# Attention and two mixtures of experts on one core: softmax reciprocals by logarithm and exponential, one pair of maxima moved, low parts of outputs moved to VectorE

## The chip, the cores and the metric

The kernel runs on 1 core of one Trainium2 chip. The metric is device time in microseconds (us), the median of three runs. A core has five engines with instruction streams of their own, each in its written order: TensorE (PE in the rows; its weight loads are PEld), VectorE (DVE), ScalarE (ACT), GpSimd (POOL) and SyncE (SP), which issues DMAs. They wait for each other by semaphores. SBUF and PSUM are the on-chip memories; matmuls write to PSUM.

## The reference

```
attention: q,k,v (2 batches, 8 heads, 1152 rows, 64 wide), fp32
  q_pool = mean of each two rows of q               # 576 rows
  scores = q_pool @ k.T / sqrt(64);  scores -= max over keys
  attn   = exp(scores);  attn /= (sum over keys + 1e-9)
  out    = attn @ v                                 # becomes x, 1152 x 512
first mixture, 4 experts, dense:  x = sum_e p_e * (relu(x @ w1[e]) @ w2[e])
second mixture, 8 experts, each row goes to its best one, times its gate
```

## The kernel before

Every value that must keep fp32 precision is split into a high part (fp32r) and a low part, the difference of the two; a product is then three matmuls: high by high, low by high, high by low.

**Jobs.** Two heads make a pair p (eight pairs); a pair has two jobs, g = 2p with 256 query columns and g = 2p+1 with 320. Even and odd below mean g. The loop `for g in range(NG)` runs the sixteen jobs in a written order, without a scheduler (`tc.manual_schedule`). A job is:

- The stream (`streams`, with `score` and `smax1`). For each of 9 key blocks and each of the two heads, four matmuls (three products and the subtraction of the maximum, `mr` by `ones`) make a score tile S, and ScalarE takes its exponential into an E tile. The two heads use the two halves of TensorE's rows and run side by side. Between them stand matmuls for the maxima of later jobs: one writes a buffer T of 384 columns, and VectorE reduces it to a maximum (L109, L110). How S and maxima (m) alternate stands in the strings `PAT`, one for each head. There are five PSUM banks for S (four named S0 to S3 and O) and three buffers T, used in turn.
- Behind the stream (called the tail below): `mT` transposes the next job's maxima into a T, and ScalarE copies them to `mr` (L130, and for odd next jobs two small copies L132). After an even job come the three tail maxima (`tops`, `tmax`, L118) into S0, S1 and a T. After an odd job come the transposes of later keys and queries (`keys`; `kT`, L65, into S0, S1 and a T; `qT`, L97, into two T).
- Then `fin(g-2)` splits the output x of the job before the last into high and low part; the low part is made on VectorE for even jobs and on GpSimd for odd ones. Then the weighted sums `av` (L174): two key blocks, then `normalise(g-1)`, then the other seven. `normalise` calls `total`, four matmuls that sum the exponentials into a T called z (L177), which ScalarE copies to r with 1e-9 added (L179); `norm(g,1)`, two reciprocals of r on VectorE (L185); and `norm(g,2)`, the product x times r (L187). `norm(g,0)` copies the weighted sum O to x (L183).

GpSimd adds up the exponentials (L168) all through attention. The list `todo` gives each job its share of the maxima of later jobs: 5 for job 0, 7 for jobs 1 to 3, 6 for jobs 4 to 13, 3 for job 14, and none for the last; each is a pair, one matmul per head.

Job 14 runs all its weighted sums ahead of `normalise(13)`. After job 15 the weights of the first mixture are split (L279 on ScalarE, L282 on VectorE), its matmuls begin (L318 to L320, then ScalarE L322 and VectorE L323 on each result), and job 15's own normalisation runs in the midst of them (`end`). From there on the kernel is the two mixtures; the change doesn't touch them.

Of the kernel before, what the change touches and what calls it, by code (L numbers as in the profile page):

```python
# [9 lines left out]
def attention(tc, q, k, v, xT, identF, prep, begin, second, keep, NJ=16):  # L10

    nc=tc.nc
    B,H,S,D=q.shape
    Q=S//2; NC=S//128; NP=NJ//2; NG=2*NP
    PAT=(("SmSSmSmSSmSmSSm","mSmSSmSmSSmSmSS"),)*2+(("SmSmSmSSmSmSSmSm","mSmSSmSmSSmSmSSm"),)
    JOB=((0,256),(256,320))
    HD=(slice(0,64),slice(64,128))
    with ExitStack() as ctx:
# [4 lines left out]
        st={}  # L23
# [9 lines left out]
        def load(p):  # L33
            b,h0=divmod(2*p,H)
            kn=ld.tile([128,NC,2,D],F32,name="kn"); qn=ld.tile([128,2,5,2,D],F32,name="qn"); vn=vp.tile([128,2,NC,D],F32,name="vn")
            st['ld',p]=kn,qn; st['v',p]=vn
            def kload(c):
                for n in range(2): nc.sync.dma_start(kn[:,c,n],k[b,h0+n].rearrange("(p c) d -> p c d",c=NC)[:,c])
            def qload(e,i0,i1):
                for n in range(2):  # L40
                    e.dma_start(qn[:,n,i0:i1],q[b,h0+n,256*i0:256*i1].rearrange("(i p r) d -> p i r d",p=128,r=2))
                    if i1==4: e.dma_start(qn[:,n,4],q[b,h0+n,896:1152].rearrange("(p r) d -> p r d",r=2))
            if p==0:
                qload(nc.scalar,0,2)
                for c in range(3): kload(slice(3*c,3*c+3))
                qload(nc.sync,2,4)
            else:
                qload(nc.sync,0,4); kload(slice(0,9))
            if p>1: load_v(p)
# [63 lines left out]
        def smax(g,i,early=False):  # L113
            for h in range(2): smax1(g,i,h,early)
# [10 lines left out]
        def mT(g):  # L125
            p,u=divmod(g,2); M=MM[u]; n=2+u; o=JOB[u][0]
            mr=st['m',g]=kq.tile([128,JOB[u][1]],F32R,name=f"mr{u}")
            f=T1(384)
            for t in range(n): nc.tensor.transpose(f[:,t*128:(t+1)*128],M[:,t].rearrange("p h d -> p (h d)"),identF)
            nc.scalar.copy(mr[:,0:256],f[:,0:256])  # L130
            if u:
                for h in range(2): nc.scalar.copy(mr[HD[h],256:320],f[HD[h],256+64*h:320+64*h])  # L132
# [42 lines left out]
        def total(g,z=None):  # L175
            n=JOB[g%2][1]; z=T1(n) if z is None else z[:,0:n]
            for h in range(2): nc.tensor.matmul(z[HD[h]],ones4,st['es',g][:,h,0:n],start=True,stop=True)  # L177
            r=st['r',g]=keep['r'] if g==NG-1 else fp.tile([128,320],F32,name="r")
            nc.scalar.activation(out=r[:,0:n],in_=z,func=AF.Identity,bias=eps)  # L179
        def norm(g,n0):  # L180
            n=JOB[g%2][1]; r=st.get(('r',g)); x=st['x',g]
            if n0==0:
                nc.scalar.copy(x[:,0:n],st['O',g][:,0:n])  # L183
            if n0==1:
                for a in range(0,n,n//2): nc.vector.reciprocal(r[:,a:a+n//2],r[:,a:a+n//2])  # L185
            if n0==2:
                nc.vector.tensor_tensor(out=x[:,0:n],in0=x[:,0:n],in1=r[:,0:n],op=ALU.mult)  # L187
        def fin(g):
            p,u=divmod(g,2); o,n=JOB[u]; b,dc=divmod(p,H//2); x=st['x',g]
            g0=b*Q+o; g1=g0+n  # L190
            while g0<g1:
                m=g0//384; e=min(g1,(m+1)*384)
                src=x[:,g0-b*Q-o:e-b*Q-o]; xh,xl=xT[m]; sl=slice(g0-384*m,e-384*m)
                nc.scalar.copy(xh[dc][:,sl],src)
                (nc.vector if g==NG-1 or u==0 and g<NG-2 else nc.gpsimd).tensor_tensor(out=xl[dc][:,sl],in0=src,in1=xh[dc][:,sl].bitcast(F32),op=ALU.subtract)
                g0=e
        load(0)
        with tc.manual_schedule():
            dw=O1(320)
            def warm(n):  # L200
                for _ in range(n): nc.tensor.matmul(dw[:,0:128],identF,identF,start=True,stop=True)
            qsum(0,slice(0,2))
            load(1)
            warm(7)
            kT(0,0); warm(1)
            qlow=qT0(0); warm(1)
            smax(0,0,True); smax(0,1,True)
            kT(0,1); st['low',0](); qlow()
            smax(0,2,True); warm(2); smax(0,3,True)
            kT(0,2); st['low',1]()  # L210
            qsum(0,slice(2,5))
            smax(0,4,True); st['low',2]()
            warm(2)
            qlow=qT0(1)
            smax(0,5,True); qlow()
            load_v(0)
            neg(0); smax(1,0); warm(3); mT(0); warm(2)
            load_v(1)
            def normalise(g): total(g); norm(g,1); norm(g,2)
            todo=[(j,i) for j in range(1,NG) for i in range(6)][1:]  # L220
            for g in range(NG):
                p,u=divmod(g,2); last=g==NG-1
                n=(5,7,7,7)[g] if g<4 else 6
                rl,todo=todo[:n],todo[n:]
                if g==0: qsum(1)
                elif u==0 and p+2<NP: load(p+2)
                elif g==NG-4: begin()
                elif u and p+2<NP: qsum(p+2)
                def between(c,hh,i):
                    if hh==1 and i==3 and c==4 and last: fin(g-2)  # L230
                streams(g,range(NC),rl,PAT[n-5],between)
                if last: break
                r=1 if g==0 else p+2 if u else NP
                def keys():
                    if r<NP:
                        for n in range(3): kT(r,n,S1(n,384) if n<2 else None)
                        qT(r)
                def tops(p):
                    if p<NP:
                        for c in range(3): tmax(p,c,S1(c,384) if c<2 else None)  # L240
                if g==0:
                    tops(0); neg(1)
                    keys(); load(2)
                    av(g,0,4); mT(1); av(g,4,NC)
                else:
                    mT(g+1)
                    if g==1: tops(1)
                    if u==0: tops(p+1)
                    keys()
                    if g>1: fin(g-2)  # L250
                    if g==NG-2: prep[0][2](); prep[3][1]()
                    c=NC if g==NG-2 else 2
                    av(g,0,c); normalise(g-1)
                    if g==NG-3:
                        for i in range(3): prep[i][1]()
                    if g==NG-2: prep[1][2]()
                    av(g,c,NC)
                norm(g,0)
            g=NG-1
            prep[2][2](); prep[3][2]()  # L260
            kqx.close(); second()
            av(g,0,NC); normalise(g-1); norm(g,0); fin(g-1)
# [635 lines left out]
```

## Time and profile before

| What | us |
|---|---|
| median of 3 runs (lowest, highest) | 773.88 (773.84, 775.05) |
| the profiled execution | 772.89 |
| its span in the profile | 771.1 |
| TensorE busy in the span | 756.8 (98%) |
| VectorE, ScalarE, GpSimd busy | 395.4, 315.0, 247.9 |

The profile is of one execution. Times in its rows count from the span's start. Attention takes the first 222 us; there VectorE is busy some 17 to 18 of every 20 us and GpSimd about 19, and in the mixtures TensorE alone is near full. Matmuls are pipelined: two that follow each other overlap in the records, so TensorE looks busy where it stalls for a few tenths, and steps from start to start tell more than durations. TensorE's granted clock is 1.00 of full speed throughout attention.

### The profile page before, as it was taken

To read this page: it belongs to the slowest core of one execution; us is meant where nothing else is said; L and a number is where in the kernel's file an instruction comes from. 1 tells how busy PE (TensorE), PEld (TensorE's weight loads), DVE (VectorE), ACT (ScalarE), POOL (GpSimd) and SP (SyncE) were. 2 spreads that over 40 slices of the span, in tenths; PEclk is the share of its full clock that TensorE was granted. 3 is DMA by queue.
4 is the path that set the end of the run, shared out by engine and by line. 5 is a ranking of instruction groups with operands and counts; after the bars stand their busy time and mean duration, and the time that the engine had idled before them with its cause. 6 is when DMAs were issued, how large, how long until landed. Compare 5 with 4: busy or idle time off the path is not lost. (4 is left out here: it accounts for less than half of the span.)

```text
span 771.1 us, 13240 instructions
## 1 busy us (share of the span) xinstructions
PE 756.8 (98%) x5166; PEld 636.9 (83%) x5166; DVE 395.4 (51%) x826; ACT 315.0 (41%) x734; POOL 247.9 (32%) x216
## 2 busy tenths in 40 slices
PE   8999999999999999999999999999999999999995
PEld 7778787877778989899898989989797978878773
DVE  6798898899594102521125212243252678474610
ACT  4757676766762212511124201132141454473611
POOL 5889999999993000000000000000000201311001
PEclk9999999999999999999999999999999999999999
DMA  8532133220063000420004000000154142797891
GB/s 225 128 97 78 20 96 98 74 97 2 9 187 134 1 1 1 158 88 1 1 0 140 26 1 1 0 1 1 42 192 151 42 164 96 274 327 301 330 371 68
DMA packets 57640, 77.54 MB, mean 101 GB/s; under 512 B 22935, under 2 KB 33175, under 8 KB 57568
## 3 DMA queue, kind: packets, MB, share of 16 engines
q1 hardware_dynamic: 55136, 70.76, 27.5%
q0 software_dynamic: 1600, 4.98, 1.9%
q8 instruction: 43, 0.70, 0.4%
q10 hardware_dynamic: 832, 0.85, 0.3%
q14 instruction: 29, 0.24, 0.1%
HBM read 71.86 MB, written 4.98 MB: 100 GB/s over the span
## 5 line engine op out<-in xcount | busy, mean ns | idle before, releaser
L322 ACT ACTIVATE hh<-ps 128x384 fp32r<-128x384 f32 x96 | 47.1, 491 | 203.9 <-PE ps L320 203.9
L318 PE MATMUL ps<-xb,w 128*128 128x384 f32 x384 | 129.6, 337 | 0.4 <-DVE hl L323 0.4
L320 PE MATMUL ps<-xb,w 128*128 128x384 f32 x384 | 128.6, 335 | 0.0
L323 DVE SCALAR_TENSOR_TENSOR hl<-ps,hh 128x384 fp32r<-128x384 f32 x96 | 53.4, 557 | 146.2 <-ACT hh L322 145.9
L468 POOL TENSOR_TENSOR r_n<-r_ss,half 128x1 f32<-128x1 f32 x9 | 5.3, 593 | 375.5 <-ACT X L467 375.5
L333 PE MATMUL py<-w,hh 128*128 128x512 f32 x288 | 112.8, 392 | 0.0
L335 PE MATMUL py<-w,hl 128*128 128x512 f32 x288 | 112.8, 392 | 0.0
L334 PE MATMUL py<-w,hh 128*128 128x512 f32 x288 | 112.7, 391 | 0.0
L319 PE MATMUL ps<-xc,w 128*128 128x384 f32 x288 | 96.7, 336 | 0.0
L282 DVE TENSOR_TENSOR w<-st,w 128x1024 fp32r<-128x1024 f32 x60 | 78.0, 1324 | 36.3 <-ACT w L279 35.2
L110 DVE TENSOR_REDUCE m<-T 128x1 f32<-128x384 f32 x180 | 88.9, 548 | 11.9 <-PE T L109 9.6
L168 POOL TENSOR_TENSOR y<-y,E 128x640 f32<-128x640 f32 x56 | 92.5, 1652 | 4.3
L143 ACT ACTIVATE E<-S 128x256 f32<-128x256 f32 (+1 forms) x240 | 84.7, 414 | 8.5 <-PE S L140 7.6
L168 POOL TENSOR_TENSOR es<-es,E 128x512 f32<-128x512 f32 x56 | 74.7, 1333 | 4.4
L174 PE MATMUL O<-E,vn 128*64 128x320 f32 (+1 forms) x576 | 75.8, 409 | 0.0
L279 ACT CAST w<-st 128x1024 fp32r<-128x1024 f32 x60 | 61.4, 1051 | 35.2 <-PE py L335 22.2
L318 PEld LDWEIGHTS ps<-xb,w 128*128 128x128 f32 x384 | 72.1, 188 | 1.9 <-issue 0.8
L320 PEld LDWEIGHTS ps<-xb,w 128*128 128x128 f32 x384 | 72.1, 188 | 0.0
L342 DVE SCALAR_TENSOR_TENSOR y<-py,p,y 128x512 f32<-128x512 f32 x27 | 20.2, 749 | 87.5 <-PE py L335 87.5
L140 PE MATMUL S<-qh,kh 64*128 64x256 f32 (+1 forms) x240 | 64.0, 303 | 0.2 <-ACT E L143 0.2
L140 PE MATMUL S<-qh,kl 64*128 64x256 f32 (+1 forms) x240 | 63.5, 301 | 0.0
L334 PEld LDWEIGHTS py<-w,hh 128*128 128x128 f32 x288 | 54.1, 188 | 11.3 <-issue 0.6
(398 smaller groups left out, 1591.4 us busy)
## 6 DMA issues: line engine op xcount, KB each, us to landing
st<-in_moe_w SPq DMA_DIRECT2D x104, 512.0 KB, 6.3
kn<-in_k SPq DMA_DIRECT2D x14, 288.0 KB, 4.6
vn<-in_v SPq DMA_DIRECT2D x14, 288.0 KB, 3.4
qn<-in_q SPq DMA_DIRECT2D x14, 256.0 KB
ysc<-y SPq DMA_DIRECT2D x9, 256.0 KB, 2.0
qn<-in_q SPq DMA_DIRECT2D x16, 64.0 KB, 4.0
kn<-in_k SPq DMA_DIRECT2D x6, 96.0 KB, 3.0
vn<-in_v ACTq DMA_DIRECT2D x2, 288.0 KB
```

Of the source, the lines that this page charges most:

```text
L110: nc.vector.tensor_reduce(out=m[:,t,h,c:c+1],in_=s,axis=AX.X,op=ALU.max)
L140: nc.tensor.matmul(s,l[hd],r[hd],start=i==0,stop=i==3)
L143: nc.scalar.activation(out=st['E',g,c][:,h,0:n],in_=s,func=AF.Exp)
L168: nc.gpsimd.tensor_tensor(out=s,in0=st['E',g,0][:,:,0:n] if c==1 else s,in1=st['E',g,c][:,:,0:n],op=ALU.add)
L174: for h in range(2): nc.tensor.matmul(O[HD[h],0:n],vn[:,h,c],st['E',g,c][:,h,0:n],start=c==0,stop=c==NC-1)
L282: def low(): (nc.vector if le=='V' else nc.gpsimd).tensor_tensor(out=wl,in0=st,in1=wh.bitcast(F32),op=ALU.subtract)
L318: nc.tensor.matmul(ps,wh[:,fs],xh[dc],start=(dc==0),stop=False)
L319: nc.tensor.matmul(ps,wh[:,fs],xl[dc],start=False,stop=False)
L320: nc.tensor.matmul(ps,wl[:,fs],xh[dc],start=False,stop=(dc==3))
L333: nc.tensor.matmul(py,hh[:,us],wh[:,cs],start=(fc==0),stop=False)
L334: nc.tensor.matmul(py,hh[:,us],wl[:,cs],start=False,stop=False)
L335: nc.tensor.matmul(py,hl[:,us],wh[:,cs],start=False,stop=(fc==7))
```

## The change

Four things are changed, all in `attention`. (1) `total` no longer copies z to r: ScalarE takes the logarithm of z + 1e-9 and then the exponential of its negative, an approximate reciprocal. `norm(g,1)` refines it by a Newton step in two VectorE instructions, the first of which writes into z, in PSUM; what they leave is the negative of the reciprocal, and `norm(g,2)` turns the sign with the product. One ScalarE function table that holds both functions is loaded at the start. (2) Of a job's pairs of maxima the last one (the sixth, or the seventh in jobs 1 to 3) is issued behind `mT` instead of in the stream; job 0, and job 14 with three, keep all in the stream. (3) The strings PAT are spaced for five or six pairs. (4) `fin` makes the low parts of jobs 1 to 11 of odd number on VectorE too; jobs 13 and 14 stay on GpSimd.

```diff
--- before.py
+++ after.py
@@ -12,7 +12,7 @@
     nc=tc.nc
     B,H,S,D=q.shape
     Q=S//2; NC=S//128; NP=NJ//2; NG=2*NP
-    PAT=(("SmSSmSmSSmSmSSm","mSmSSmSmSSmSmSS"),)*2+(("SmSmSmSSmSmSSmSm","mSmSSmSmSSmSmSSm"),)
+    PAT=(("SmSSmSSmSSmSSm","mSSmSSmSSmSSmS"),("SmSSmSmSSmSmSSm","mSmSSmSmSSmSmSS"))
     JOB=((0,256),(256,320))
     HD=(slice(0,64),slice(64,128))
     with ExitStack() as ctx:
@@ -176,15 +176,19 @@
             n=JOB[g%2][1]; z=T1(n) if z is None else z[:,0:n]
             for h in range(2): nc.tensor.matmul(z[HD[h]],ones4,st['es',g][:,h,0:n],start=True,stop=True)
             r=st['r',g]=keep['r'] if g==NG-1 else fp.tile([128,320],F32,name="r")
-            nc.scalar.activation(out=r[:,0:n],in_=z,func=AF.Identity,bias=eps)
+            st['z',g]=z
+            nc.scalar.activation(out=r[:,0:n],in_=z,func=AF.Ln,bias=eps)
+            nc.scalar.activation(out=r[:,0:n],in_=r[:,0:n],func=AF.Exp,scale=-1.0)
         def norm(g,n0):
             n=JOB[g%2][1]; r=st.get(('r',g)); x=st['x',g]
             if n0==0:
                 nc.scalar.copy(x[:,0:n],st['O',g][:,0:n])
             if n0==1:
-                for a in range(0,n,n//2): nc.vector.reciprocal(r[:,a:a+n//2],r[:,a:a+n//2])
+                z=st['z',g]
+                nc.vector.scalar_tensor_tensor(out=z,in0=z,scalar=1e-9,in1=r[:,0:n],op0=ALU.add,op1=ALU.mult)
+                nc.vector.scalar_tensor_tensor(out=r[:,0:n],in0=z,scalar=-2.0,in1=r[:,0:n],op0=ALU.add,op1=ALU.mult)
             if n0==2:
-                nc.vector.tensor_tensor(out=x[:,0:n],in0=x[:,0:n],in1=r[:,0:n],op=ALU.mult)
+                nc.vector.scalar_tensor_tensor(out=x[:,0:n],in0=x[:,0:n],scalar=-1.0,in1=r[:,0:n],op0=ALU.mult,op1=ALU.mult)
         def fin(g):
             p,u=divmod(g,2); o,n=JOB[u]; b,dc=divmod(p,H//2); x=st['x',g]
             g0=b*Q+o; g1=g0+n
@@ -192,9 +196,10 @@
                 m=g0//384; e=min(g1,(m+1)*384)
                 src=x[:,g0-b*Q-o:e-b*Q-o]; xh,xl=xT[m]; sl=slice(g0-384*m,e-384*m)
                 nc.scalar.copy(xh[dc][:,sl],src)
-                (nc.vector if g==NG-1 or u==0 and g<NG-2 else nc.gpsimd).tensor_tensor(out=xl[dc][:,sl],in0=src,in1=xh[dc][:,sl].bitcast(F32),op=ALU.subtract)
+                (nc.gpsimd if NG-4<g<NG-1 else nc.vector).tensor_tensor(out=xl[dc][:,sl],in0=src,in1=xh[dc][:,sl].bitcast(F32),op=ALU.subtract)
                 g0=e
         load(0)
+        nc.scalar.preload_act_table_set("natural_log_exp_and_others")
         with tc.manual_schedule():
             dw=O1(320)
             def warm(n):
@@ -228,7 +233,8 @@
                 elif u and p+2<NP: qsum(p+2)
                 def between(c,hh,i):
                     if hh==1 and i==3 and c==4 and last: fin(g-2)
-                streams(g,range(NC),rl,PAT[n-5],between)
+                late=rl[n-1:] if g else []
+                streams(g,range(NC),rl[:n-1] if g else rl,PAT[n==7],between)
                 if last: break
                 r=1 if g==0 else p+2 if u else NP
                 def keys():
@@ -244,6 +250,7 @@
                     av(g,0,4); mT(1); av(g,4,NC)
                 else:
                     mT(g+1)
+                    for z in late: smax(*z)
                     if g==1: tops(1)
                     if u==0: tops(p+1)
                     keys()
```

TensorE, at the end of job 6's stream and before its weighted sums, before the change: T_1914 is the stream's last maximum, T_1921 the transposes, S0, S1 and T_1935 the tail maxima.

```order
L140 MATMUL S2_1906<-ql_1234,kh_1214 128x256
L109 MATMUL T_1914<-kh_1677,qh_1696 128x384 [waits DVE_49]
L140 MATMUL S2_1906<-mr0_1671,ones_146 128x256
L129 MATMUL T_1921<-identF_61,MM1_151 128x128 [waits DVE_49]
L129 MATMUL T_1921<-identF_61,MM1_151 128x128 x2
L118 MATMUL S0_1928<-kh_1677,qt0_152 128x384 [waits Activation_49]
L118 MATMUL S1_1932<-kh_1677,qt0_152 128x384 [waits Activation_49]
L118 MATMUL T_1935<-kh_1677,qt0_152 128x384 [waits DVE_49]
L174 MATMUL O_1940<-E_1766,vn_808 64x256 [waits DMAHW4_49]
```

The same place after the change; T_1914 is the last maximum of the stream, T_1921 the transposes, T_1928 and T_1931 the pair, S0, S1 and T_1941 the tail maxima.

```order
L140 MATMUL S2_1906<-ql_1237,kh_1217 128x256
L109 MATMUL T_1914<-kh_1682,qh_1701 128x384 [waits DVE_49]
L140 MATMUL S2_1906<-mr0_1670,ones_146 128x256
L129 MATMUL T_1921<-identF_61,MM1_151 128x128 [waits DVE_49]
L129 MATMUL T_1921<-identF_61,MM1_151 128x128 x2
L109 MATMUL T_1928<-kh_1682,qh_1701 128x384 [waits DVE_49]
L109 MATMUL T_1931<-kh_1682,qh_1701 128x384 [waits DVE_49]
L118 MATMUL S0_1934<-kh_1682,qt0_152 128x384 [waits Activation_49]
L118 MATMUL S1_1938<-kh_1682,qt0_152 128x384 [waits Activation_49]
L118 MATMUL T_1941<-kh_1682,qt0_152 128x384 [waits PE_49,Activation_49]
L174 MATMUL O_1946<-E_1772,vn_810 64x256 [waits DMAHW4_49]
```

The pair stands between the transposes and the tail maxima, each half with a wait for VectorE; the third tail maximum, which waited for VectorE, now waits for ScalarE (Activation) as well as for TensorE.

VectorE, in the tail of job 7, before the change: kl and ql are low parts of later keys and queries, x_1941 the output of job 6.

```order
L73 TENSOR_TENSOR kl_2141<-T_2153,kh_2140 128x384 [waits Activation_49]
L100 SCALAR_TENSOR_TENSOR ql_2160<-T_2161,qh_2159 128x512 [waits Activation_49]
L100 SCALAR_TENSOR_TENSOR ql_2160<-T_2166,qh_2159 128x64 [waits Activation_49]
L185 RECIPROCAL r_2187<-r_2187 128x128 [waits Activation_49]
L185 RECIPROCAL r_2187<-r_2187 128x128
L187 TENSOR_TENSOR x_1941<-x_1941,r_2187 128x256 [waits DVE_49,Pool_49]
```

And after it; x_1721 is the output of job 5, x_1947 that of job 6, T_2191 is z.

```order
L73 TENSOR_TENSOR kl_2148<-T_2160,kh_2147 128x384 [waits Activation_49]
L100 SCALAR_TENSOR_TENSOR ql_2167<-T_2168,qh_2166 128x512 [waits Activation_49]
L100 SCALAR_TENSOR_TENSOR ql_2167<-T_2173,qh_2166 128x64 [waits Activation_49]
L199 TENSOR_TENSOR xc0_99<-x_1721,xb0_98 128x128 [waits Activation_49]
L199 TENSOR_TENSOR xc1_101<-x_1721,xb1_100 128x192 [waits Activation_49]
L188 SCALAR_TENSOR_TENSOR T_2191<-T_2191,r_2194 128x256 [waits DVE_49,PE_49,Activation_49]
L189 SCALAR_TENSOR_TENSOR r_2194<-T_2191,r_2194 128x256 [waits DVE_49]
L191 SCALAR_TENSOR_TENSOR x_1947<-x_1947,r_2194 128x256 [waits DVE_49]
```

Two low parts come in ahead, the two reciprocals became two steps that read and write z and r, and the product follows as before.

ScalarE, between job 14's transposes and job 15's stream, before the change: w and st are weights, T_3744 is the total of job 13, x_3725 the weighted sum of job 14, E_3763 the first exponentials of job 15.

```order
L279 CAST w_3146<-st_3139 128x1024 [waits DMAHW1_49]
L179 ACTIVATE r_3747<-T_3744,y4_111 128x320 [waits PE_49]
L183 COPY x_3725<-O_3724 128x256 [waits Pool_49]
L143 ACTIVATE E_3763<-S0_3754 128x320 [waits PE_49]
L143 ACTIVATE E_3763<-S1_3756 128x320 [waits PE_49]
```

And after it.

```order
L286 CAST w_3158<-st_3151 128x1024 [waits DMAHW1_49]
L180 ACTIVATE r_3761<-T_3758,y4_111 128x320 [waits PE_49]
L181 ACTIVATE r_3761<-r_3761 128x320 [waits Activation_49]
L185 COPY x_3739<-O_3738 128x256
L143 ACTIVATE E_3778<-S0_3769 128x320 [waits PE_49,Pool_49]
L143 ACTIVATE E_3778<-S1_3771 128x320 [waits PE_49]
```

One more instruction stands ahead of job 15's first exponential, and it waits for the one before it.

## Rows read from the trace of the kernel before

**Rows 1.** Streams 0-3, 5-7, 11, 12, 14, 15: stretch, length, busy PE, PEld, DVE, ACT, POOL.

```profile
15.08:21.00 5.92, 5.78 (x84) 5.40 (x83) 4.93 (x10) 4.97 (x18) 5.23 (x5) 1.00 0.70 207
28.57:35.46 6.89, 6.86 (x88) 6.57 (x86) 6.16 (x14) 6.26 (x18) 5.31 (x5) 1.00 0.06 12
44.15:50.63 6.48, 6.45 (x89) 5.87 (x87) 6.21 (x16) 5.86 (x19) 4.02 (x4) 1.00 0.85 237
56.20:63.62 7.42, 7.15 (x88) 6.65 (x86) 7.23 (x15) 6.37 (x18) 7.26 (x6) 1.00 0.00 0
...
82.66:89.36 6.70, 6.70 (x86) 6.44 (x85) 6.02 (x14) 6.07 (x18) 6.46 (x7) 1.00 0.00 0
96.68:102.81 6.13, 6.13 (x87) 5.68 (x85) 5.51 (x13) 5.20 (x17) 5.89 (x7) 1.00 0.83 238
108.39:115.35 6.96, 6.96 (x87) 6.44 (x85) 6.73 (x14) 6.16 (x18) 6.80 (x6) 1.00 0.00 0
...
160.16:167.32 7.16, 7.16 (x86) 6.47 (x85) 6.89 (x15) 6.15 (x18) 7.00 (x6) 1.00 0.01 2
174.64:181.35 6.71, 6.71 (x87) 5.90 (x85) 6.68 (x15) 5.34 (x17) 6.47 (x6) 1.00 0.01 4
...
199.66:205.19 5.53, 5.53 (x80) 5.18 (x78) 3.22 (x8) 5.12 (x17) 5.37 (x5) 1.00 0.01 3
210.25:216.71 6.46, 6.31 (x75) 5.45 (x73) 5.75 (x5) 6.35 (x19) 6.15 (x5) 1.00 0.25 84
```

**Rows 2.** Timeline of TensorE in job 15: start, length, what, idle before and releaser.

```profile
210.94 0.30 PE L140 MATMUL S<-qh,kh 64*128 64x320 f32 x2
...
211.38 0.30 PE L140 MATMUL S<-mr,ones 64*128 64x320 f32 x2
```

**Rows 3.** Timeline, first mixture: TensorE, then VectorE.

```profile
228.31 0.34 PE L320 MATMUL ps<-xb,w 128*128 128x384 f32 x1
229.07 0.44 PE L318 MATMUL ps<-xb,w 128*128 128x384 f32 x1 [0.42 <-DVE hl L323]
...
225.93 1.75 DVE L185 RECIPROCAL r<-r 128x128 f32<-128x128 f32 x2
```

**Rows 4.** TensorE, the end of job 7.

```profile
114.95 0.34 PE L109 MATMUL T<-kh,qh 64*128 64x384 f32 x1
...
115.35 0.44 PE L129 MATMUL T<-identF,MM 128*128 128x128 f32 x2
...
117.24 1.03 PE L174 MATMUL O<-E,vn 128*64 128x320 f32 x6
```

**Rows 5.** VectorE, the read of the last maximum in that stream.

```profile
115.34 0.56 DVE L110 TENSOR_REDUCE m<-T 128x1 f32<-128x384 f32 x1 [0.19 <-PE T L109]
```

**Rows 6.** TensorE, the end of job 6.

```profile
102.81 0.55 PE L129 MATMUL T<-identF,MM 128*128 128x128 f32 x3
103.11 0.60 PE L118 MATMUL S<-kh,qt 128*128 128x384 f32 x2
...
103.82 1.08 PE L174 MATMUL O<-E,vn 128*64 128x256 f32 x8
```

**Rows 7.** ScalarE, copies of the transposed maxima in that tail.

```profile
103.39 0.37 ACT L130 CAST mr<-T 128x256 fp32r<-128x256 f32 x1
103.66 0.42 ACT L132 CAST mr<-T 64x64 fp32r<-64x64 f32 x2
```

**Rows 8.** Groups of VectorE by line and shape, 56 to 200 us: busy, mean ns, idle.

```profile
L185 DVE RECIPROCAL r<-r 128x160 f32<-128x160 f32 x11 | 11.9, 1116 | 0.6 <-ACT r L179 0.5
L187 DVE TENSOR_TENSOR x<-x,r 128x320 f32<-128x320 f32 x6 | 6.0, 1005 | 0.2
...
L73 DVE TENSOR_TENSOR kl<-T,kh 128x384 fp32r<-128x384 f32 x5 | 2.7, 547 | 0.0
...
L195 DVE TENSOR_TENSOR xc<-x,xb 128x64 fp32r<-128x64 f32 x1 | 1.3, 1295 | 0.0
```

**Rows 9.** ScalarE, first exponentials of job 15.

```profile
211.13 1.10 ACT L143 ACTIVATE E<-S 128x320 f32<-128x320 f32 x3
```

## The prediction

> **What bounds the kernel now.** I read the page first, then a table of the attention's score streams by job, then the order of events at the end of a stream, then the groups of VectorE. A job is half of a pair of heads; there are sixteen, 0 to 15, even ones with 256 query columns and odd ones with 320. In [rows 1] each line is one stream, from its first score matmul to the first transpose behind it. TensorE is busy for the whole stretch in nearly every line, so attention is a chain on TensorE; but its records overlap and hide short stalls, so the lengths must be compared with what the matmuls need. In [rows 2] two 320-column matmuls start 0.44 us and three steps apart: 0.147 us for each of the two halves of the array, which run side by side. A stream has 36 such matmuls per half and 6 maxima of 384 columns (0.147 x 384 / 320 = 0.176): 5.29 + 1.06 = 6.35 us. Jobs 5 and 9 take 6.70 and 6.72 (the first in [rows 1], the second like it), so a stream has 0.35 over for its start and end; jobs 7 and 11 take 6.96 and 7.16, so they lose 0.3 to 0.5 more. For 256 columns one step is 0.118, so 4.23 + 1.06 + 0.35 = 5.64, but job 6 takes 6.13, and three more even jobs (4, 8, 10) take 6.13 or 6.14. Half a microsecond is lost there because VectorE needs about 0.5 us for each of the twelve maxima, over 6 us, and a score matmul for a maximum must wait until one of three buffers T has been read. Job 14, with six maxima instead of twelve, takes 5.53; that is what ScalarE's eighteen exponentials allow.
>
> Behind attention TensorE runs the first mixture of experts without a gap but one: at 228.31 to 229.07 [rows 3] it steps 0.76 where 0.17 is usual, because VectorE comes to the first low part only after the reciprocals that began at 225.93.
>
> **One pair of maxima leaves the stream.** Jobs 1 to 13 now keep five pairs (six in jobs 1 to 3) and put one pair behind the transposes that end the stream. In the stream this gives:
> Even jobs 4, 6, 8, 10: 4.23 + 0.88 + 0.35 = 5.46 by TensorE, but 5.53 by job 14; I take 5.55, a gain of 0.58 each.
> Odd jobs: 5.29 + 0.88 + 0.35, about 6.50: gains of 0.20 (jobs 5 and 9), 0.46 (job 7, and job 13 like it) and 0.66 (job 11).
> Jobs 1, 2, 3 still have six pairs there, instead of seven: about 6.70, 6.13 and 6.70, gains of 0.19, 0.35 and 0.72.
> Job 0 only has its five pairs spaced evenly: 5.55 for 5.92, a gain of 0.37. Job 12 loses time to small vector work of its own and goes to perhaps 5.65, a gain of 1.06.
>
> **What the pair costs where it lands.** It needs two T buffers. The order shows three in turn: the last two maxima of the stream, the transposes, then the pair, so the second matmul of the pair waits until the stream's very last maximum has been read. In job 7 that matmul starts at 114.95, 0.40 before the transposes [rows 4], and its read runs from 115.34 for 0.56 us [rows 5], to 0.55 after the transposes began. So the second matmul goes at about +0.6 and ends at +0.77, where the next work began at +0.30 before [rows 6]. In odd jobs all that follows moves by 0.47 to 0.5; nothing is nearer there, since the key transposes go to other banks.
> In even jobs three matmuls of the tail maxima follow, of 0.17 each; by the pair alone the weighted sums would begin at +0.77 + 0.51 = +1.28, for +1.01 in job 6 [rows 6]. But the third of them now takes the T that the transposes used, and waits for ScalarE's copies of it: the last of these starts at 103.66 and, with 0.42 for two, ends 1.27 after the transposes began [rows 7]. So +1.33 + 0.17 = +1.50, which is 0.49 more than before. These copies stand behind ScalarE's exponentials, which end no sooner by the change.
> Bounds: below, the pair costs only its own 0.2 (two halves side by side, T free in time); above, 1.0, if the reads are a full maximum later. I take 0.5, the sum of events.
>
> Net, gain minus 0.49: jobs 4, 6, 8, 10 gain 0.09 each (0.36); job 12 gains 0.57; job 2 loses 0.14. Odd, minus 0.50: jobs 5 and 9 lose 0.30 each, job 7 loses 0.04, job 13 gains nothing that counts, job 11 gains 0.16, job 3 gains 0.22. Job 1 loses 0.5: its tail maxima and key transposes take turns on the same banks behind VectorE, so I put 0.7 for the pair there. Job 0 gains 0.37. Sum of these: a gain of 0.36 + 0.57 + 0.16 + 0.22 + 0.37 = 1.68 against losses of 0.14 + 0.60 + 0.04 + 0.50 = 1.28: 0.4 us gained.
>
> **The reciprocals.** Two reciprocals of 160 columns take 1.116 each [rows 8], 2.2 us per odd job, and 1.75 the two of 128 [rows 3]. In their place stand two steps that read PSUM and SBUF; the nearest row, 384 columns from the same places, takes 0.547 [rows 8]. For 256 and 320 columns I take 0.45 and 0.5 (bounds 0.4 and, as for the product with both inputs in SBUF, 1.0): VectorE saves 0.85 and 1.2 per job. It lies beside the weighted sums on TensorE, with the pair's 1.1 us and the moved low parts to fill it again, so it is worth nothing of itself. On ScalarE one more exponential per job, about 0.44, falls where ScalarE waits for the weighted sums: hidden. The buffer z stays in use until the second step has read it, which is before the third maximum of the next stream wants it. ScalarE's function table is loaded once, as before.
> Two places have no cover. Job 15's stream is bound by ScalarE (6.46 with no maximum at all [rows 1], where the matmuls need 5.29 + 0.35), and the total before it now has logarithm and exponential ahead of its first softmax exponential at 211.13 [rows 9]; that one starts later by one operation and its latency: 0.5 us lost (bounds 0.33, the spacing of three in 1.10, and 0.6). And at 225.93 VectorE has two short steps instead of 1.75 us, so the first low part comes 0.85 earlier, more than the 0.59 that TensorE loses: 0.59 gained (bounds 0 and 0.59).
>
> **The low parts moved from GpSimd to VectorE.** Six odd jobs, 1 to 11, one or two pieces each, beside the weighted sums. On VectorE these have both inputs in SBUF, and there the time is uncertain: a piece of only 64 columns took 1.295 us [rows 8], and the product of 320 columns took 1.005 in the mean for a bare 0.5. I take 0.5 to 1.3 a piece. In job 7's tail, from the transposes: last read to +0.55, pair to +1.8, key and query low parts to +4.4, low parts to +6.2, the two steps to +7.2, the product to +8. The next stream begins at +7.8 and has three T buffers, so VectorE may be late by 1.6 before TensorE notices. Cost taken: nothing. GpSimd loses about 1 us of work per pair of jobs; it is late in its sums but nobody waits for it, so that is worth nothing either.
> The Trainium skill says, in its page "SBUF — State Buffer" under "Who interferes with whom", that a VectorE instruction with two SBUF inputs contends with a GpSimd instruction that reads SBUF, and that the second to issue waits for the whole of the first. The 64-column piece at 1.295 agrees; by that rule each moved piece can meet a GpSimd add, while the two Newton steps, with one input in PSUM, meet none. It is what the second rival is made of.
>
> **Sum.** 0.4 - 0.5 + 0.59 = 0.5 us gained. The profiled execution took 772.89, so 772.4; the median shown is 0.99 above that execution, so on its scale 773.88 - 0.5 = 773.4.
>
> **Rivals.** First, the pair is as good as free. It speaks for it that its two matmuls use different halves of the array; against it stand the waits in the order, on VectorE for both and on ScalarE for the third tail maximum. Then the six even jobs 2 to 12 gain 0.29 more and the seven odd ones 0.3 more: 1.7 + 2.1 = 3.8, so 769.6.
> Second, slower: the moved low parts are blocked at 1.3 a piece, 2.6 for two pieces, and the product at 1.5, so in odd tails VectorE ends at +9.4 instead of +8, 1.6 into the next stream. That is the point from which it decides: from there the even streams wait for T buffers as they do now and stay at 6.13 or above. Five even streams then give back 0.58 and job 1's successor 0.35, and the tails' own products add some: 3.2, so 773.4 + 3.2 = 776.6. For it: those long pieces in [rows 8]. Against it: ten maxima at 0.5 leave VectorE room to catch up in a stream.
>
> **How the numbers follow.** A measurement of this kernel can't tell 0.2% (1.55 us) from nothing; so the three outcomes split at 772.3 and 775.4. Forecast, with its own range 772.0 to 775.0: 0.42. First rival: 0.36. Second: 0.22. A part of the forecast falls over either edge and a part of each rival falls short of its own: faster 0.37, same 0.41, slower 0.22. The range reaches to both rivals' values, 769.5 to 776.7, which leaves out about 2 in 10 together with a cost above the bounds.
>
> **What would show it.** In the profile after: even streams near 5.55 and odd ones near 6.5; the second late maximum about 0.6 behind the transposes, and the weighted sums at +1.5 (even) and +2.4 (odd; +1.89 now [rows 4]). Two steps of about 0.5 instead of the reciprocals; no stall near 228; job 15's first exponential half a microsecond later. I am wrong if the pair starts at once behind the transposes (faster), or if VectorE's product ends beyond 1.6 us into an even stream (slower).

## The result, and the profile after

The changed kernel takes 779.04 us (median of five runs, 778.62 to 779.37), the kernel before 773.88 beside it: ratio 1.0064, 95% interval 1.0049 to 1.008, slower. The forecast was 773.4 with a range to 776.7, so it was wrong. The profiled span is 777.3 for 771.1, 6.2 us longer; the medians differ by 5.2, since the profiled execution of the kernel before took 0.99 less than its median.

The streams of the changed kernel, with the same columns as [rows 1] (jobs 0, 1, 5, 6, 7, 11, 12, 14, 15):

```profile
15.08:20.96 5.88, 5.82 (x83) 5.36 (x82) 4.60 (x10) 4.97 (x18) 5.19 (x5) 1.00 0.75 221
28.54:36.06 7.52, 6.78 (x86) 6.44 (x85) 6.21 (x13) 6.78 (x19) 5.90 (x6) 1.00 0.02 5
...
85.13:91.56 6.43, 6.43 (x84) 6.24 (x82) 5.00 (x10) 5.85 (x18) 6.27 (x6) 1.00 0.00 0
99.67:105.51 5.84, 5.81 (x85) 5.40 (x83) 4.63 (x11) 5.21 (x18) 4.71 (x4) 1.00 0.82 239
111.88:118.32 6.44, 6.44 (x85) 6.25 (x83) 5.00 (x10) 5.86 (x18) 6.28 (x6) 1.00 0.00 0
...
165.43:171.87 6.44, 6.44 (x84) 6.25 (x83) 5.73 (x12) 5.86 (x18) 6.28 (x6) 1.00 0.03 5
179.97:186.50 6.53, 6.22 (x84) 5.65 (x82) 6.36 (x15) 5.41 (x18) 5.25 (x5) 1.00 0.01 3
...
205.74:211.50 5.76, 5.73 (x80) 5.21 (x78) 3.32 (x8) 5.22 (x18) 5.53 (x5) 1.00 0.01 3
216.56:223.43 6.87, 6.70 (x74) 5.49 (x73) 5.63 (x5) 6.72 (x20) 6.63 (x5) 1.00 0.30 85
```

All but those of jobs 1, 14 and 15 became shorter. Over the sixteen jobs the streams gain 3.6 us, where I had forecast 6.5. What lies between a stream and the next (the tail) loses 10.3, where I had forecast 6.6. The start of the first mixture moves from 222.13 to 228.86, and 0.5 comes back behind it.

TensorE at the end of job 6 (answers to [rows 6]), then VectorE's reads of the pair there; in these rows `64*128` is a matmul on half of the array's rows and `128*128` one on the whole array:

```profile
105.51 0.55 PE L129 MATMUL T<-identF,MM 128*128 128x128 f32 x3
105.99 0.67 PE L109 MATMUL T<-kh,qh 64*128 64x384 f32 x2
106.58 0.62 PE L118 MATMUL S<-kh,qt 128*128 128x384 f32 x2
107.04 0.34 PE L118 MATMUL T<-kh,qt 128*128 128x384 f32 x1
107.31 0.44 PE L174 MATMUL O<-E,vn 128*64 128x256 f32 x2
...
106.47 1.02 DVE L110 TENSOR_REDUCE m<-T 128x1 f32<-128x384 f32 x2 [0.31 <-PE T L109]
```

The pair begins 0.48 behind the transposes, the tail maxima 1.07 (0.30 before), the weighted sums 1.80 (1.01 before): +0.79. The third tail maximum starts 0.46 behind the first (0.44 before), without a wait for ScalarE. TensorE's weight loads there (PEld), two rows after the change and one before it:

```profile
105.98 0.41 PEld L109 LDWEIGHTS T<-kh,qh 64*128 64x128 f32 x2 [0.17 <-issue]
106.58 0.30 PEld L118 LDWEIGHTS S<-kh,qt 128*128 128x128 f32 x2 [0.18 <-issue]
...
103.09 0.36 PEld L118 LDWEIGHTS S<-kh,qt 128*128 128x128 f32 x2
```

After the change the weight loads sit idle 0.17 ahead of the pair and 0.18 ahead of the tail maxima, with no releaser in the profile. Before it the tail maxima's weights were loaded behind the transposes without a gap. TensorE at the end of job 7 (answers to [rows 4]), then VectorE there, from its reads of the pair to the product:

```profile
118.32 0.44 PE L129 MATMUL T<-identF,MM 128*128 128x128 f32 x2
118.69 0.71 PE L109 MATMUL T<-kh,qh 64*128 64x384 f32 x2
119.32 0.88 PE L65 MATMUL S<-identF,kn 128*128 128x128 f32 x6
...
121.00 0.49 PE L174 MATMUL O<-E,vn 128*64 128x320 f32 x2
...
119.16 1.02 DVE L110 TENSOR_REDUCE m<-T 128x1 f32<-128x384 f32 x2 [0.26 <-PE T L109]
...
122.65 1.91 DVE L199 TENSOR_TENSOR xc<-x,xb 128x128 fp32r<-128x128 f32 x2
124.49 0.42 DVE L188 SCALAR_TENSOR_TENSOR T<-T,r 128x256 f32<-128x256 f32 x1
124.94 0.42 DVE L189 SCALAR_TENSOR_TENSOR r<-T,r 128x256 f32<-128x256 f32 x1
125.40 0.86 DVE L191 SCALAR_TENSOR_TENSOR x<-x,r 128x256 f32<-128x256 f32 x1
```

Weighted sums at +2.68 for +1.89: again +0.79. VectorE's product ends at +7.94, ahead of the next stream. The tails of jobs 3 to 12 are all 0.76 to 0.80 longer, those of jobs 1, 2 and 13 by 0.94, 0.90 and 0.62. In job 1 TensorE, then VectorE:

```profile
36.06 0.44 PE L129 MATMUL T<-identF,MM 128*128 128x128 f32 x2 [0.74 <-DVE MM L123]
...
35.84 0.17 DVE L123 TENSOR_REDUCE MM<-m 128x4 f32<-128x12 f32 x1
```

Of job 1's pairs the first six are all of job 2's maxima. With only six in the stream the last of them stands at its very end, and the transposes wait 0.74 for it. ScalarE ahead of job 15 (answers to [rows 9]), and VectorE's first low part in the mixture (answers to [rows 3]):

```profile
217.23 0.47 ACT L181 ACTIVATE r<-r 128x320 f32<-128x320 f32 x1
...
217.86 1.42 ACT L143 ACTIVATE E<-S 128x320 f32<-128x320 f32 x4
...
234.10 0.55 DVE L330 SCALAR_TENSOR_TENSOR hl<-ps,hh 128x384 fp32r<-128x384 f32 x1
```

Job 15's first exponential stands 1.30 behind the start of its stream, 0.88 before; the stream is 0.41 longer. The first low part of the mixture now comes 5.24 behind the mixture's start (6.34 before), early enough that no stall of TensorE is left there.

### The profile page after: what moved, and what is told of

Read it like the earlier page. It is cut to its first block, busy times and chain, and to the rows that moved or that the text cites. A ratio compares the mean times of both kernels' runs of the same rounds, so it can differ in the third digit from the quotient of the medians.

```text
span 777.3 us, 13261 instructions
## 1 busy us (share of the span) xinstructions
PE 761.8 (98%) x5166; PEld 638.9 (82%) x5166; DVE 395.2 (51%) x836; ACT 321.2 (41%) x750; POOL 242.8 (31%) x206
## 5 line engine op out<-in xcount | busy, mean ns | idle before, releaser
L110 DVE TENSOR_REDUCE m<-T 128x1 f32<-128x384 f32 x180 | 92.7, 553 | 26.5 <-PE T L109 23.5
L289 DVE TENSOR_TENSOR w<-st,w 128x1024 fp32r<-128x1024 f32 x60 | 79.6, 1350 | 35.6 <-ACT w L286 34.8
L143 ACT ACTIVATE E<-S 128x256 f32<-128x256 f32 (+1 forms) x240 | 82.9, 416 | 8.0 <-PE S L140 7.2
L341 PEld LDWEIGHTS py<-w,hh 128*128 128x128 f32 x288 | 54.1, 188 | 11.2 <-issue 0.6
L174 PEld LDWEIGHTS O<-E,vn 128*64 128x64 f32 x576 | 39.8, 137 | 28.5 <-issue 2.8
L340 PEld LDWEIGHTS py<-w,hh 128*128 128x128 f32 x288 | 54.1, 188 | 11.1 <-ACT hh L329 0.5
```

What stands on the lines that cost most here:

```text
L110: nc.vector.tensor_reduce(out=m[:,t,h,c:c+1],in_=s,axis=AX.X,op=ALU.max)
L143: nc.scalar.activation(out=st['E',g,c][:,h,0:n],in_=s,func=AF.Exp)
L174: for h in range(2): nc.tensor.matmul(O[HD[h],0:n],vn[:,h,c],st['E',g,c][:,h,0:n],start=c==0,stop=c==NC-1)
L289: def low(): (nc.vector if le=='V' else nc.gpsimd).tensor_tensor(out=wl,in0=st,in1=wh.bitcast(F32),op=ALU.subtract)
L340: nc.tensor.matmul(py,hh[:,us],wh[:,cs],start=(fc==0),stop=False)
L341: nc.tensor.matmul(py,hh[:,us],wl[:,cs],start=False,stop=False)
```

## The experiments

Theory P: the moved pair alone makes the kernel slower. Rival L: the low parts hold up VectorE. Ratios are to the kernel before, run beside each, with 95% intervals; "faster" and "slower" mean that the interval leaves out 1.

**Pair put back**, all else as in the changed kernel.

```
-    PAT=(("SmSSmSSmSSmSSm",...              +    PAT=(("SmSSmSmSSmSmSSm",... (as before)
-    streams(g,range(NC),rl[:n-1] if g ...   +    streams(g,range(NC),rl,PAT[n-5],between)
-    for z in late: smax(*z)
```

> The changed kernel with the pair of maxima put back into the stream and the strings PAT of before; the reciprocals by logarithm and exponential and the low parts on VectorE stay. Theory P (the moved pair is what costs: after the change the tails behind the streams are 0.79 us longer in jobs 2 to 12, 5.58 to 6.38 in even ones and 7.32 to 8.11 in odd ones, which is more than the streams got shorter): the tails go back to 5.58 and 7.32 and the time to 771 to 773.5. Rival L (the low parts on VectorE, and the longer way to the reciprocal, hold TensorE up): the time stays at 777 to 779.

Measured: 773.62, ratio 1.0012 (0.9997 to 1.0028). Tails are back at 5.58 and 7.32, as by P. But job 12's stream takes 9.17; VectorE, GpSimd, then TensorE there:

```profile
171.20 0.18 DVE L855 TENSOR_REDUCE pz<-pd 128x9 f32<-128x36 f32 x1
171.41 1.30 DVE L856 TENSOR_SCALAR pz<-pz 128x9 f32<-128x9 f32 x1
...
173.20 1.18 DVE L858 TENSOR_TENSOR p<-pd,pz 128x36 f32<-128x36 f32 x1
...
171.01 1.68 POOL L168 TENSOR_TENSOR y<-y,E 128x640 f32<-128x640 f32 x1
...
174.85 0.41 PE L109 MATMUL T<-kh,qh 64*128 64x384 f32 x1 [0.61 <-DVE r L189]
```

An operation on 9 columns takes 1.30 us. It is one of four small operations on the experts' shares: three of them, behind a low part of 1.47, stand ahead of the first Newton step, and the fourth (1.18) stands between the two steps. z keeps its T until the second step (L189), and a maximum of the stream waits for it. The product behind ends 2.9 us into the stream, and only then does VectorE read the stream's first maximum.

**Pair alone moved**, in the kernel before, with the changed strings.

```
+    late=rl[n-1:] if g else []
+    streams(g,range(NC),rl[:n-1] if g else rl,PAT[n==7],between)
+    for z in late: smax(*z)                  (behind mT)
```

> The kernel before with only the pair moved behind the transposes and the new strings PAT; reciprocals and low parts as before. Theory P: 778 to 780, tails of 6.3 to 6.4 and 8.0 to 8.1. Rival L: 771 to 774, tails as before.

Measured: 781.67, ratio 1.012 (1.01 to 1.014). Tails are 6.38 and 8.1 and most streams 5.85 and 6.43, as in the changed kernel: P holds. But the time is above the 778 to 780 of P, and the loss above that of the whole change: the streams of jobs 11 and 13 take 7.86 and 7.16 (6.44 and 6.45 in the changed kernel). VectorE's product, behind the old reciprocals, ends 2.8 and 2.1 us into them. I had not expected that.

**Pair in other banks**, still behind the transposes: first half into S3, second into O, which wait for no maximum.

```
-    s=S1(h+i%2*2,384) if early else T1(384)
+    s=(S1(3,384) if h==0 else O1(384)) if early=='late' else S1(...) if early else T1(384)
```

> The changed kernel with the pair at the same place, but written to the PSUM banks S3 and O, which are free there, instead of two buffers T. Theory P says that the 0.79 is made of a wait for a buffer T (the second matmul of the pair goes when the stream's last maximum has been read, about 0.3 after the first) and of TensorE going twice more between matmuls on the whole array and on its halves (about 0.2 each). Then this takes away the wait alone: tails shorter by 0.25 to 0.35, 775 to 776.5. If the wait is all, tails lose 0.6 and the time is 771 to 772. Rival L: 779.

Measured: 779.32, ratio 1.009 (1.0069 to 1.0112). TensorE at the end of job 6:

```profile
104.56 0.55 PE L129 MATMUL T<-identF,MM 128*128 128x128 f32 x3
105.04 0.44 PE L109 MATMUL S<-kh,qh 64*128 64x384 f32 x1
105.04 0.44 PE L109 MATMUL O<-kh,qh 64*128 64x384 f32 x1
105.41 0.62 PE L118 MATMUL S<-kh,qt 128*128 128x384 f32 x2
...
106.59 1.08 PE L174 MATMUL O<-E,vn 128*64 128x256 f32 x8 [0.39 <-DVE m L110]
```

The halves now start together. Still the pair begins 0.48 behind the transposes, where a tail maximum began at 0.30, and the tail maxima come 0.37 after that for a matmul that needs 0.17: +0.55 without a wait for a T (S3 and O were free 0.7 us earlier, when the last exponential that reads O ended). In odd tails the key transposes come at +0.73 (1.00 in the changed kernel, 0.28 before). So the wait for T is 0.22 to 0.27 and the rest 0.45 to 0.55. Even tails are longer here (6.61 for 6.38), since the weighted sums wait for O until VectorE has read the maximum in it. So the time misses the 775 to 776.5 expected, and the size of the wait is read from the rows.

**Pair ahead of the transposes**, same banks.

```
+    for z in late: smax(*z,'late')
     mT(g+1)
-    for z in late: smax(*z,'late')
```

> As the run with the pair in banks S3 and O, but with the pair ahead of the transposes, right behind the stream, where TensorE works on its halves already. Theory P with both parts: only the pair's own matmul time of about 0.2 stays, tails of about 5.8 and 7.5, 771 to 773. If going between whole and half arrays costs nothing: the same as with the pair behind the transposes in those banks. Rival L: 779.

Measured: 774.04, ratio 1.002 (1.0011 to 1.003), a little above the 771 to 773 expected. TensorE at the end of job 7:

```profile
114.72 0.31 PE L140 MATMUL S<-mr,ones 64*128 64x320 f32 x1
114.78 0.34 PE L109 MATMUL S<-kh,qh 64*128 64x384 f32 x1
114.87 0.34 PE L109 MATMUL O<-kh,qh 64*128 64x384 f32 x1
115.14 0.44 PE L129 MATMUL T<-identF,MM 128*128 128x128 f32 x2
```

Here the pair follows score matmuls of its own kind, `64*128`: the stream with it takes 6.61 for 6.43, and the tail is 7.32 again. Even streams take 6.05 for 5.85, but even tails 6.00, not 5.58: as in the run above, the weighted sums wait for O. By the place alone, stream and tail together go from 14.28 to 13.94 in job 7 and from 12.45 to 12.05 in job 6. The same two matmuls cost 0.18 among half-array work and 0.45 to 0.55 between `128*128` work. The Trainium skill says, in its page "TensorEngine Tiling (Array Packing)" under "Key Properties", that a change of tiling mode drains TensorE; these runs agree, at 0.3 to 0.4 us for in and out. That it is the draining, and not something else in the change from one kind to the other, they do not show.

**Low parts alone**, in the kernel before.

```
-    (nc.vector if g==NG-1 or u==0 and g<NG-2 else nc.gpsimd).tensor_tensor(out=xl...
+    (nc.gpsimd if NG-4<g<NG-1 else nc.vector).tensor_tensor(out=xl...
```

> The kernel before with one edit: the low parts of jobs 1 to 11 of odd number on VectorE. Theory P (the moved pair alone makes the kernel slower): the low parts cost little, 772 to 775 against about 773.5 for the kernel before, streams 4, 6, 8, 10 at 6.13 as before; most of any loss in job 12, where the run with the pair put back showed a stream of 9.2 instead of 6.7. Rival L (the low parts hold up VectorE, and that is the loss): 777 or more, with tails unchanged and odd streams 0.3 to 0.6 longer, since the reciprocals are still long here.

Measured: 775.9, ratio 1.0041 (1.0029 to 1.0052). The streams of jobs 4 and 12 (columns as in [rows 1]):

```profile
70.21:77.04 6.83, 6.75 (x86) 5.90 (x85) 6.80 (x14) 5.39 (x17) 5.56 (x5) 1.00 0.91 239
174.81:182.11 7.30, 6.75 (x87) 5.90 (x85) 7.23 (x17) 5.38 (x17) 6.65 (x6) 1.00 0.01 2
```

VectorE fills both. Job 4 went from 6.13, job 12 from 6.71; jobs 8 and 10 lose 0.2, job 15 0.4, jobs 6 and 9 nothing, and job 7 wins 0.25. L is a real cost (3.2 us, a little above what P allowed), but a third of the pair's 9.2, each moved alone.

**Reciprocals alone**, in the kernel before (edit 1 of the change only).

```
-    nc.scalar.activation(out=r[:,0:n],in_=z,func=AF.Identity,bias=eps)
+    nc.scalar.activation(out=r[:,0:n],in_=z,func=AF.Ln,bias=eps)
+    nc.scalar.activation(out=r[:,0:n],in_=r[:,0:n],func=AF.Exp,scale=-1.0)    (and the Newton step)
```

> The kernel before with one edit: the reciprocals by logarithm, exponential and two steps; low parts, pairs and strings as before. Both theories: faster than before by 0.5 to 2.5, 771 to 773. In numbers by stage: streams of jobs 7 and 11 from 6.96 and 7.16 to 6.7 (0.7 in all, with job 13), job 12 at 6.7 or a little above instead of the 9.2 of the run with the low parts on VectorE, job 15 longer by 0.4 (6.88), 0.5 won at the start of the first mixture. If job 12 is at 9 here too, it is the new reciprocals and not the low parts that hold it up.

Measured: 770.31, ratio 0.9959 (0.9943 to 0.9974), faster, and by more than expected: job 12 alone gains 0.56, where I had expected nothing. Streams of jobs 7, 12 and 15:

```profile
107.82:114.54 6.72, 6.72 (x86) 6.45 (x85) 6.05 (x14) 6.08 (x18) 6.49 (x7) 1.00 0.01 2
...
173.32:179.47 6.15, 6.15 (x86) 5.69 (x85) 6.10 (x14) 5.21 (x17) 5.91 (x5) 1.00 0.02 4
208.13:215.01 6.88, 6.70 (x74) 5.49 (x72) 5.65 (x6) 6.73 (x20) 6.57 (x5) 1.00 0.26 88
```

Jobs 7 and 12 were at 6.96 and 6.71 [rows 1]; job 11 goes from 7.16 to 6.71, and jobs 3 and 13 gain 0.63 and 0.23. All five were streams into which VectorE came late: in the kernel before, its product ended 1.3 to 1.6 us into them.

**Other strings** in the changed kernel.

```
-    PAT=(("SmSSmSSmSSmSSm","mSSmSSmSSmSSmS"),
+    PAT=(("SmSSmSSmSSmSSm","mSmSSmSSmSSmSS"),
```

> The changed kernel with one edit: in the strings for five pairs the second head's maxima stand a place away from the first head's (SmSSmSSmSSmSSm beside mSmSSmSSmSSmSS). If the even streams stay at 5.85 instead of 5.55 because both halves of a pair come at nearly one time and take two buffers together, they go to 5.55 to 5.65, and job 14 from 5.76 back to 5.53: 1.2 to 1.7 won, about 777.5. If they stay at 5.85, it is VectorE's load as such, and the time stays at 779.

Measured: 776.4, ratio 1.005 (1.0029 to 1.0071). Streams of jobs 4 and 14:

```profile
72.58:77.98 5.40, 5.40 (x84) 5.26 (x82) 4.68 (x11) 4.99 (x17) 4.05 (x4) 1.00 0.81 240
...
203.44:208.88 5.44, 5.44 (x80) 5.16 (x78) 3.31 (x8) 5.13 (x18) 5.28 (x4) 1.00 0.01 3
```

Job 4 went from 5.85, job 14 from 5.76: the strings cost 0.3 to 0.45 in six even streams (jobs 0, 4, 6, 8, 10 and 14); job 12 stays at 6.52. The mixture starts 2.6 us earlier; of that the ratios (1.005 beside 1.0064) show 1.1, which their intervals don't tell apart. The reason I had written down is wrong: in job 6 the maxima come two and two here as well, and closer (0.18 to 0.22 us apart; 0.36 to 0.58 in the changed kernel). What differs is that with these strings the second head always stands one maximum behind the first, while with the changed ones it falls back and catches up, so that scores of both heads come at the same moment. That this is the cause was read from the strings and starts, not tested.

**Pair back, small operations later**: the first run, with the four operations on the experts' shares moved into the first mixture and job 13 normalised by reciprocals.

```
+    if t0 and b==0 and fc==5: share()                      (in the first mixture; out of job 12)
+    if g==NG-3: nc.scalar.activation(out=r[:,0:n],in_=z,func=AF.Identity,bias=eps); return
```

> The changed kernel with pair and strings as before (773.6), and two more edits: the four small VectorE operations on the shares of the experts moved from job 12 into the first mixture, and job 13's normalisation by plain reciprocals. If the 2.5 lost in job 12's stream come from these small operations beside GpSimd, job 12 goes to 6.7 or less (from 9.2) and job 15 back to 6.46 (from 6.88): 770 to 771. If the low parts themselves hold VectorE up there, job 12 stays above 8 and the time at 773.

Measured: 771.09, ratio 0.9979 (0.9963 to 0.9995). Job 12 takes 6.14 and job 15 6.52: the low part stays there and costs nothing alone. With the reciprocals alone the small operations stay and cost nothing either (6.15): the 3 us need both. Job 13's normalisation was changed together with this; it comes behind job 12's stream.

**Reciprocals, job 0 and job 15 mended.**

```
+    if g==NG-3: nc.scalar.activation(out=r[:,0:n],in_=z,func=AF.Identity,bias=eps); return
+    PAT=(("SmSSmSSmSSmSSm","mSmSSmSSmSSmSS"), ...           (five pairs: job 0)
```

> The kernel with the new reciprocals alone (770.3), and two more edits: job 13's total copied and inverted by plain reciprocals as before, so that ScalarE has one operation and not two ahead of job 15's first exponential, and job 0's five pairs staggered. If the 0.4 of job 15 comes from that operation, its stream goes from 6.88 to 6.5; if job 0 follows the staggered strings of the earlier run, from 5.91 to 5.58. Sum 0.7: 769.6, and less than 0.2 of a gain if neither holds.

Measured: 771.2, ratio 0.9972 (0.9961 to 0.9984). Job 0 takes 5.56 and job 15 6.60, so the mixture starts 0.74 earlier than with the reciprocals alone, but the time isn't shorter: in its profiled execution the second mixture waits 0.95 us for a DMA of weights and 0.94 for a split. Whether an earlier start is always spent there stays open.

**Pair ahead, strings and reciprocals, low parts on GpSimd as before**; job 1 keeps seven pairs in its stream.

```
+    s=S1(3,384) if early=='late' and h==0 else T1(384) if early=='late' else ...
+    kk=n-1 if g>1 else n; late=rl[kk:] if g else []
```

> As the kernel before it, plus the pair of maxima moved, but ahead of the transposes, where it follows half-array matmuls, one half in S3 and one in a T buffer; strings for five pairs staggered; job 1 keeps its seven pairs in the stream; low parts on GpSimd as before. If the loss behind the transposes is the change between whole-array and half-array matmuls plus the wait for a T, the pair costs about 0.2 here and the tails are as before: even jobs 5.40 + 0.20 + 5.58 = 11.2 instead of 11.7, odd jobs 6.36 + 0.18 + 7.32 = 13.9 instead of 14.0, so 766 to 767. If the pair costs 0.5 or more wherever it stands, even tails are at 6.0 or more or streams at 5.9, and the time is 769 to 771.

Measured: 774.37, ratio 1.002 (1.0009 to 1.0031), a miss. Even jobs take 5.57 + 5.58 and odd ones 6.53 + 7.33, as expected, and job 1 is back at 6.90 + 8.68. But jobs 9 and 11 have tails of 7.64 and 8.87, and job 15's stream takes 10.19. ScalarE, then GpSimd there, and TensorE in job 11's tail:

```profile
213.18 0.77 ACT L143 ACTIVATE E<-S 128x320 f32<-128x320 f32 x2 [1.45 <-POOL es L168]
...
205.78 11.77 POOL L168 TENSOR_TENSOR es<-es,E 128x512 f32<-128x512 f32 x6
...
165.60 0.66 PE L97 MATMUL T<-identF,qs 128*128 128x128 f32 x4 [1.33 <-POOL qs L58]
```

The exponentials wait for GpSimd's sums: with TensorE faster, GpSimd has become the one that is late. In job 11's tail it is the same: the transposes of later queries wait 1.33 for GpSimd's sums of queries (`qs`).

**The same with the low parts on VectorE** and the small operations later: two edits together.

```
-    (nc.vector if g==NG-1 or u==0 and g<NG-2 else nc.gpsimd).tensor_tensor(out=xl...
+    (nc.gpsimd if NG-4<g<NG-1 else nc.vector).tensor_tensor(out=xl...
+    if t0 and b==0 and fc==5: share()
```

> The run with the pair ahead of the transposes and everything else (774.4), with the low parts of odd jobs 1 to 11 on VectorE again and the four small operations on the shares of the experts out of job 12. There GpSimd had become late: ScalarE waited in job 15 for sums of exponentials (stream 10.2 instead of 6.5) and tails of jobs 9 and 11 were 0.3 and 1.6 longer. If that is GpSimd's load, these three go, job 15's stream is at 6.5 to 7 and the even jobs stay at 5.57 + 5.58: the first mixture starts at about 218.5 to 219.5, and 768 to 769.5. If VectorE then is the one that is late, even streams go back to 5.8 or more, and the time stays at 771 or above.

Measured: 766.02, ratio 0.9914 (0.99 to 0.9927): faster than both kernels. Streams of jobs 6, 7, 12 and 15:

```profile
94.72:100.29 5.57, 5.57 (x87) 5.38 (x85) 4.81 (x12) 5.17 (x18) 5.33 (x5) 1.00 0.81 239
105.87:112.39 6.52, 6.52 (x86) 6.29 (x85) 5.38 (x12) 5.95 (x18) 6.29 (x7) 1.00 0.01 3
169.82:175.39 5.57, 5.57 (x86) 5.38 (x84) 4.80 (x12) 5.16 (x18) 5.33 (x4) 1.00 0.01 3
203.79:210.31 6.52, 6.37 (x74) 5.45 (x72) 5.81 (x5) 6.37 (x19) 6.21 (x5) 1.00 0.30 84
```

Here a pair in the stream's end is part of each length; the tails are 5.58 and 7.33. The mixture starts at 215.74, for 222.13 before and 228.86 in the changed kernel. That is 2.8 earlier than expected: job 15's weighted sums, which had waited for the exponentials too, take 5.4 for 8.0. Of the two edits only the low parts take work from GpSimd, so I put its being in time down to them; neither was run alone on that kernel. Against "pair back, small operations later" (771.09, ratio 0.9979), from which this kernel differs by the pair ahead of the transposes and the strings alone, it wins 5 us: the pair and its strings pay here.

**And job 13 by the new reciprocals.**

```
-    if g==NG-3: nc.scalar.activation(out=r[:,0:n],in_=z,func=AF.Identity,bias=eps); return
```

> The same, with job 13's normalisation by logarithm, exponential and two steps like the others, so that VectorE is freed of two reciprocals beside the splitting of weights, and ScalarE has one operation more ahead of job 15's first exponential. By that operation alone job 15's stream is 0.3 to 0.4 longer than in the run beside it; if VectorE's splitting of weights decides, the later part is shorter by as much.

Measured: 766.59, ratio 0.9915 (0.9902 to 0.9929). Job 15 takes 6.87 for 6.52 as expected; the time is not told apart from the run beside it.

## Why the prediction was wrong, step by step

The profiled span missed by 6.7 us (0.5 shorter forecast, 6.2 longer measured): 3.7 of it lies in the tails, 2.9 in the streams.

**What the pair costs where it lands** is the step that failed. I put 0.49 and 0.5; it is 0.79 in most tails, even and odd alike. The second late maximum came where I had put it (+0.63 in job 7 for "about +0.6"), but the next work starts 0.37 behind it, where I allowed 0.17. And the wait for the T, from which I worked out the whole, is worth only 0.22 to 0.27: so much came back in the run without it. I took the pair's own cost as 0.17 to 0.2, what it costs in a stream; between the whole-array transposes and tail maxima it is 0.45 to 0.55. The rows showed which matmuls use half the array (`64*128`) and which the whole, and [rows 6] showed whole following whole at 0.30; I didn't ask what changing over would cost, and put it at nothing. The wait for ScalarE that made up the last 0.2 of my 0.49 in even tails didn't occur.

**Even streams.** 5.85 instead of 5.55, 0.2 to 0.3 in six of them (jobs 0, 4, 6, 8, 10, 14): the strings, as the other strings showed with 5.40 to 5.44 (5.58 in job 0). I counted the maxima and took them to be well spread. The gain by counting was there, but not with these strings. The 5.40 is also below the 5.53 of job 14 that I had read as what ScalarE allows: it was no such bound. Nor do twelve maxima need "over 6 us" of VectorE: [rows 1] show it busy for 5.51 of job 6's 6.13. What held the streams of six pairs at 6.13 was read from the rows and not tested.

**Job 1.** 1.57 lost instead of 0.5: the stream lost 0.63 where I had forecast a gain of 0.19, and the tail 0.94 for 0.7. I had looked at its tail, not at which maximum the transposes wait for. The kernel that leaves job 1 alone has none of it.

**Job 12.** 6.53 instead of 5.65: with the pair alone moved it takes 5.84, so I put the 0.7 down to the low part beside the small operations, by the 3 us that the two cost with the pair put back. VectorE's product ends 2.1 us into this stream. That is where "cost taken: nothing" failed; into no other stream is the product later than 1.1 us, and in job 7's tail it ended at +7.94 for my +8.

**Right were** the odd streams (6.43 for 6.50), job 15 (+0.41 for 0.5), the steps (0.42 and 0.49 for 0.45 and 0.5) and the start of the mixture (0.5 for 0.59). But the credit was misplaced: "worth nothing of itself" was said of the reciprocals on VectorE, and alone they win 2.4 us, most of it in the streams of jobs 3, 7, 11, 12 and 13, whose gain I had credited to the pair.

**Rivals.** The second rival named the right side and came nearest (776.6), but by luck: its mechanism, VectorE late by the low parts, is only the 0.7 of job 12; the even streams are at 5.85, not at 6.13. Of my two signs of being wrong, the pair did not start at once, and a product beyond 1.6 us into an even stream came in job 12 alone: the loss came by a way that neither named. The first rival's premise, that the two halves run side by side and are as good as free, holds ahead of the transposes only, where the pair costs 0.18 to 0.20.

## What to carry to other kernels

Price a moved instruction by its new neighbours, not by what it cost in its old place: on TensorE look whether they use the same part of the array. A change of several parts is a sum only as long as no part is what another needs: the reciprocals won alone, the pair lost where it stood and won a few instructions earlier (with other strings and with VectorE and GpSimd in time), and the low parts went with a gain only where TensorE had become fast enough for GpSimd to be late. When work leaves a full stream, look also at how the rest is spread, and at what stands last there.

## What the runs showed of the hardware

Two half-array matmuls of 384 columns cost 0.18 us among their own kind and 0.45 to 0.55 between whole-array matmuls, with no wait for a T; in the rows of jobs 6 and 7 the weight loads sat idle 0.17 to 0.19 us at each change from one to the other. And of two small operations of VectorE that started within one add of GpSimd (171.01 to 172.69), a `TENSOR_REDUCE` took 0.18 us and a `TENSOR_SCALAR` on 9 columns 1.30, to 172.71, as the add ended. The Trainium skill's page "SBUF — State Buffer", under "Who interferes with whom", lists `tensor_scalar` among the operations that can contend with GpSimd for a shared pair of ports, and says that the one to issue second is blocked for the whole of the other's instruction; these rows agree.
